# Converting float64 weights on ScalarE and VectorE alone, in pieces of 544 columns

## The chip, the core and the metric

The kernel runs on one core of a Trainium2 chip. The core's engines work side by side, each through its own list of instructions in order: TensorE (PE; its weight loads are shown apart as PEld), VectorE (DVE), ScalarE (ACT), GpSimd (POOL) and SyncE (SP), which here issues all transfers. They wait for each other by semaphores. The metric is the device time of one execution in microseconds.

## The reference

Attention with sketched features, and behind it one block that mixes tokens. `S1` and `S2` (8 x 32) and the four weight matrices of the second block come in as float64, `q`, `k`, `v` as float32.

```python
# B, H, S, D = 4, 4, 1088, 32; r = 8
def phi(x):                                   # 64 features of a token
    a, b = x @ S1.T, x @ S2.T
    return outer(a, b).reshape(64)
kv  = phi(k).T @ v                            # per batch and head
num = phi(q) @ kv
den = phi(q) @ sum(phi(k)) + 1e-6
x   = (num / den), heads side by side         # [B, 1088, 128]
theta = x @ w_theta
y   = w_tok_r @ (x * cos(theta)) + w_tok_i @ (x * sin(theta))   # over the 1088 tokens
u   = x + y
out = u + relu(u @ w_ch)
```

## The kernel before

Tokens are handled in 9 chunks of 128, three chunks to a group, so three groups a batch. For each batch, `keys(b)` cuts `k` and `q` into bfloat16 slices (`sl_k`, `sl_q`), sums `k k'` exactly, carries this through two more small products (their slices are `gsl`, `tsl`, `nsl`) into `rq`, with which the slices of `q` are multiplied later, and sums the features of `k` with `v` into `kvbd`. This is a long chain of small steps that goes to and fro between VectorE, ScalarE (casts, L196), GpSimd (remainders `r`, `r_c`) and TensorE. `queries(b, g)` works on a group: slices of `q` times `rq` give `lv` (ScalarE), then VectorE starts with `hi<-lv`, finds the denominator, the numerator, `x`, and theta's reduced angle (`tn`, `tt`), ScalarE takes sine and cosine, and `z` holds x cos and x sin. `mix(b, g)` multiplies all 17 tiles of `z` with a third of the columns of `wT`, the token weights (L509, product `y`), and finishes the output rows.

`wT` has 17 row blocks (`NK`) of 128 x 1088 float32. It is made once, at the beginning, from `w_tok`, which lies in memory as float64, by `load_f32` (L105). `load_f32` takes a piece of 272 columns (`part = S // 4`, so 68 pieces): a transfer brings the float64 words into a staging tile `st` (pool `stg`, six buffers); ScalarE takes the absolute value of each high word (L99) and turns the low word into a rounding step (L116, in place in `st`); VectorE clamps and shifts the magnitude (L84, twice); GpSimd adds the step as an integer (L80); VectorE masks a bit (L84) and puts the sign back from `st` (L87). `w2`, the two square matrices, goes the same way in one piece of 256 columns.

The program calls `tokens(20)` between the first batch's groups and the rest behind `keys(1)`, but that is not the order in which the engines run them: a scheduler of the compiler places every instruction in its engine's list by the costs and due times that it computes, and so the four VectorE passes of a piece stand far apart and among other work. It orders the transfers on SyncE's queue too. All buffers are handed out in turn, and a writer waits until the last reader of that buffer is done.

Of the kernel before, what the change touches and what calls it, by code (L numbers as in the profile page):

```python
"""Polysketch attention followed by the WaveMLP phase block, one launch on one core.

The float inputs that come in as float64 are handed to the chip as their bits (int64) and turned
into float32 there; S1 and S2 become pairs of float32.

The attention's denominator q' M q, M = S1' S1 (sum k k') S2' S2, comes close to zero, so it is
computed to about 2^-35 of its terms: every factor is cut into bfloat16 slices on a fixed grid, whose
products the tensor engine adds up exactly in float32, level by level (a level is the sum of
the two slices' numbers). Everything else is float32.
"""  # L10
# [9 lines left out]
F32 = mybir.dt.float32  # L20
BF16 = mybir.dt.bfloat16
I32 = mybir.dt.int32
U32 = mybir.dt.uint32
# [6 lines left out]
P = 128  # L30
EXPO = 0x7F800000          # a float32's exponent
SIGN = -(1 << 31)
SLICE = 1.5 * 2.0**17      # times 2^e: rounds values under 2^(e+1) to 8 bits and a sign
NL = 5                     # levels kept
ROUND = 1.5 * 2.0**23      # rounds to whole numbers
TWO_PI_A = 6.28125         # 2 pi, its first 8 bits and the rest
TWO_PI_B = 2.0 * math.pi - TWO_PI_A
PI_LOW = 3.1415925


@with_exitstack
def kernel(
    ctx: ExitStack,
    tc: tile.TileContext,
    q: bass.AP,       # [B, 128, NC, H, D], token 128 c + p, zeros behind the last
    k: bass.AP,
    v: bass.AP,
    s_t: bass.AP,     # [D, 2, R]: S1', S2'
    s_2: bass.AP,     # [R, D]: S2
    w_sq: bass.AP,    # [128, 2, 128]: w_theta, w_ch  # L50
    w_tok: bass.AP,   # [2 NF + 1, 128, S]: rows of w_tok_r', w_tok_i', and the last rows of both
    out: bass.AP,     # [B, S, 128]
):
# [12 lines left out]
    const = ctx.enter_context(tc.tile_pool(name="const", bufs=1))  # L66
    stg = ctx.enter_context(tc.tile_pool(name="stg", bufs=6))
    ld = ctx.enter_context(tc.tile_pool(name="ld", bufs=1))
# [10 lines left out]
    def tt(eng, o, a, b, op):  # L79
        eng.tensor_tensor(out=o, in0=a, in1=b, op=op)  # L80

    def ts(o, a, s1, op0, s2=None, op1=None):
        kw = {} if op1 is None else {"op1": op1}
        V.tensor_scalar(out=o, in0=a, scalar1=s1, scalar2=s2, op0=op0, **kw)  # L84

    def stt(o, a, s, b, op0, op1):
        V.scalar_tensor_tensor(out=o, in0=a, scalar=s, in1=b, op0=op0, op1=op1)  # L87
# [3 lines left out]

# [1 line left out]
    def split(t):  # L93
# [3 lines left out]
    def magnitude(h, hi):  # L97
        """The exponent and upper mantissa at float32's places, bits 30 and 31 not yet right."""
        A.activation(h, hi.bitcast(F32), AF.Abs)  # L99
        ts(h, h, 2.0**-15, ALU.max)  # L100
        x = h.bitcast(I32)
        ts(x, x, 3, ALU.logical_shift_left)
        return x

    def load_f32(dst, src):  # L105
        """dst [p, n] in SBUF = src, rounded to nearest."""
        p, n = dst.shape
        if src.dtype == F32:
            nc.sync.dma_start(dst, src)
            return  # L110
        st = stg.tile([P, n], I64, tag="st", name="st")[:p]
        nc.sync.dma_start(st, src)
        lo, hi = split(st)
        x = magnitude(dst, hi)
        # 2.0 + round(lo / 2^29) steps: its bits add the rounded low part and turn bit 30.
        A.activation(lo.bitcast(F32), lo.bitcast(U32), AF.Copy, bias=2.0, scale=2.0**-51)  # L116
        tt(G, x, x, lo, ALU.add)
        ts(x, x, 0x7FFFFFFF, ALU.bitwise_and)
        stt(x, hi, SIGN, x, ALU.bitwise_and, ALU.bitwise_or)

    def load_pair(src, n, tag, copies=1):
        """src as float32 pairs hi + lo, each [copies * p, n]."""
        p = src.shape[0]
# [23 lines left out]

# [1 line left out]
    ident = const.tile([P, P], F32, tag="ident", name="ident")  # L149
# [8 lines left out]
    def powers(m, n):  # L158
        """m [128, n], not negative: the greatest power of two up to each column's maximum."""
        t = psum(ps_acc, "acc")  # L160
        nc.tensor.transpose(t[:n, :P], m, ident)
        mx = sm.tile([P, 1], F32, tag="mx", name="mx")[:n]
        V.tensor_reduce(out=mx, in_=t[:n, :P], axis=AX.X, op=ALU.max)
        ts(mx.bitcast(I32), mx.bitcast(I32), EXPO, ALU.bitwise_and)
        dg = sm.tile([P, 2 * H], F32, tag="dg", name="dg")[:n, :n]
        ts(dg, ident[:n, :n], mx, ALU.mult)
        o = psum(ps_acc, "acc")
        nc.tensor.matmul(o[:, :n], ones[:n, :], dg, start=True, stop=True)
        s = sm.tile([P, 2 * H], F32, tag="pw", name="pw")[:, :n]
        V.tensor_copy(s, o[:, :n])  # L170
        return s

    def grids(pw, n, bits=8):
        """Numbers that round to the first and the second slice's grid."""
        g = sm.tile([P, 2, 2 * H], F32, tag="grid", name="grid")
        first = SLICE * 2.0 ** (8 - bits)
        ts(g[:, 0, :n], pw, first, ALU.mult)
        ts(g[:, 1, :n], pw, first * 2.0**-8, ALU.mult)
        return g
# [4 lines left out]
    def cut(cols, src, dst, r, g, lo=None, p=P):  # L184
        """Slices of src (+ lo). cols: (index into the grid, view) pairs, where view takes the
        part of a tile that has that scale; dst: the slices' tiles, r: a scratch tile."""
        for i, gi in ((0, 0), (1, 1)):
# [12 lines left out]
    def levels(src, n, by_head=False):  # L200
        """The sum hi + lo of the NL levels, src in PSUM: [p, NL, n], or [p, H, NL, n / H]."""
        lv = sm.tile([P, NL, n], F32, tag="lev", name="lev")
        A.copy(lv.rearrange("p l (h r) -> p h l r", h=H) if by_head else lv, src)
# [9 lines left out]

# [1 line left out]
    tiles = {}  # L215
# [6 lines left out]

# [1 line left out]
    load(0)  # L224
# [19 lines left out]
    V.tensor_copy(s1c, ssl[:, :, 0:R])  # L244
    # S2 with its rows on partitions: slices, and these four times side by side.
    s2sl = const.tile([P, NL, D], BF16, tag="s2sl", name="s2sl")[:R]
# [3 lines left out]
    for i in range(4):  # L250
        V.tensor_copy(s2x[:, :, i], s2sl)
    # S2' S2 by levels, its slices four times side by side.
    pp = psum(ps_acc, "acc")[:, :NL * D]
# [33 lines left out]

# [1 line left out]
    def keys(b):  # L289
# [15 lines left out]

        # Sums of k k' by slices: exact in the first ones.
        gp = psum(ps_acc, "acc")
# [13 lines left out]

        # (S1 C)' by levels, then N' = (S1 C P)'.
        tp = psum(ps_acc, "acc")[:, :H * NL * R]
# [57 lines left out]

# [1 line left out]
    def queries(b, g):  # L383
# [26 lines left out]

        # a . g, each cut into two slices of 11 bits on a grid of the token's own and a rest.
        def pair(x):
# [34 lines left out]

        # The numerator.
        qp = work.tile([P, CH, R, R], F32, tag="feat", name="qp")
# [20 lines left out]

        # theta, brought to [-pi, pi]; cos is sin(pi / 2 - |theta|).
        tr = psum(ps_tr, "tr")
# [5 lines left out]
        for i in range(GC):  # L478
            nc.tensor.matmul(th[:, i * P:(i + 1) * P], xT[:, i * P:(i + 1) * P], w2[:, 0],  # L479
                             start=True, stop=True)  # L480
        n_ = work.tile([P, GC * P], F32, tag="tn", name="tn")
        t_ = work.tile([P, GC * P], F32, tag="tt", name="tt")
        ts(n_, th, 1.0 / (2.0 * math.pi), ALU.mult, ROUND, ALU.add)
# [17 lines left out]

# [1 line left out]
    def mix(b, g):  # L503
# [25 lines left out]

# [1 line left out]
    load_f32(w2.rearrange("p t n -> p (t n)"), w_sq.rearrange("p t n -> p (t n)"))  # L531
    keys(0)
    queries(0, 0)
    part = S // 4
    pieces = [(i, n) for i in range(NK) for n in range(4)]

# [4 lines left out]

    tokens(20)
    queries(0, 1)
    tokens(20)
    queries(0, 2)
    tokens(20)
    load(1)
# [54 lines left out]
```

## Time and profile before

| | |
|---|---|
| median of 3 runs | 555.96 us (555.05 to 556.31) |
| span of the profiled execution, first to last instruction | 551.7 us |
| the profiled execution's own time | not recorded apart; the median is 4.3 us above the span |
| busy: TensorE / its weight loads | 338.5 us (61%) / 245.6 us (45%) |
| busy: VectorE / ScalarE / GpSimd | 393.4 us (71%) / 174.3 us (32%) / 164.7 us (30%) |
| mean granted TensorE clock | 0.759 |
| transfers | 28.93 MB, mean 52 GB/s |

Busy shares are averages over stages with different limits, so they say little by themselves. In the views, `out<-in` names the tiles an instruction writes and reads, L105 is line 105 of the kernel, "idle before" is the time in which the engine stood still ahead of an instruction, and the name behind the arrow is what ended it. In the tables of stretches, `(x30)` counts instructions and PEclk is the granted TensorE clock as a share of full speed.

### The profile page before, as it was taken

What the parts mean: (1) busy time and instruction counts of PE and PEld (TensorE: products, weight loads), DVE (VectorE), ACT (ScalarE), POOL (GpSimd) and SP (SyncE); (2) the same over time, 40 slices, a digit from 0 to 9 for tenths busy, and PEclk for the clock granted to TensorE, in tenths of its full rate; (3) what the DMA queues carried; (4) which work ended last, traced back from release to release, by engine and by line L of the source; (5) the groups of instructions that cost most, each with busy time, mean ns of one, the idle gap of its engine ahead of it and who ended that gap; (6) DMA issues with size and microseconds to landing.
All of it is one profiled execution on the core that took longest, in us unless ns stands there. A gap on an engine that the chain in (4) does not pass through costs nothing.

```text
span 551.7 us, 6346 instructions
## 1 busy us (share of the span) xinstructions
PE 338.5 (61%) x1971; PEld 245.6 (45%) x1971; DVE 393.4 (71%) x1207; ACT 174.3 (32%) x418; POOL 164.7 (30%) x209
## 2 busy tenths in 40 slices
PE   3212216345476625795677489956964997677696
PEld 2202106333354313564544357645644575545364
DVE  5988998888989989978679765186697541677311
ACT  3313443645635432304414221044144112234100
POOL 1315644453456524311321431021226110122000
PEclk9999555557676956697686669976687899586799
DMA  7022343542323542001001011000000000000000
GB/s 250 21 62 85 103 122 101 165 119 65 113 71 102 180 120 70 23 7 55 2 0 44 0 45 57 15 12 1 1 1 1 1 15 27 1 1 0 1 14 26
DMA packets 16513, 28.93 MB, mean 52 GB/s; under 512 B 1760, under 2 KB 6112, under 8 KB 16480
## 3 DMA queue, kind: packets, MB, share of 16 engines
q1 hardware_dynamic: 16480, 28.53, 16.8%
q8 instruction: 15, 0.25, 0.2%
q14 instruction: 18, 0.15, 0.1%
HBM read 26.30 MB, written 2.23 MB: 52 GB/s over the span
## 4 chain that ended last, share of the span: by engine, by line
DVE 43%; PE 33%; POOL 9%; issue 7%; ACT 5%; DMA 2%; SPq 1%; DVEq 0%; POOLq 0%; ACTq 0%
PE y L509 15%; DVE wT L84 8%; DVE wT L87 5%; DVE s L80 4%; POOL pr L80 4%; PE acc L366 4%; DVE r L80 3%; DVE qp L80 2%; PE mm L479 2%; POOL wT L80 2%; PE mm L518 2%; POOL r L80 2%; DVE sl_q L84 2%; DVE dn L441 2%; PE tr L474 1%
## 5 line engine op out<-in xcount | busy, mean ns | idle before, releaser
L509 PE MATMUL y<-wT,z 128*128 128x384 f32 (+1 forms) x408 | 159.0, 534 | 48.7 <-DVE z L80 30.5
L509 PEld LDWEIGHTS y<-wT,z 128*128 128x128 f32 x408 | 81.2, 213 | 90.2 <-DVE z L80 32.1
L84 DVE TENSOR_SCALAR wT<-wT 128x272 int32<-128x272 int32 (+1 forms) x204 | 78.2, 419 | 6.1 <-POOL wT L80 6.0
L80 POOL TENSOR_TENSOR wT<-wT,st 128x272 int32<-128x272 int32 x68 | 61.4, 912 | 69.9 <-DVE wT L84 43.7
L99 ACT ACTIVATE wT<-st 128x272 f32<-128x272 f32 x68 | 30.6, 449 | 37.4 <-DMA st<-w_tok 36.9
L80 DVE TENSOR_TENSOR uT<-xT,y 128x384 f32<-128x384 f32 (+1 forms) x12 | 6.3, 528 | 42.2 <-PE y L509 42.2
L80 POOL TENSOR_TENSOR z<-x,tt 128x384 f32<-128x384 f32 (+1 forms) x12 | 14.1, 1177 | 73.3 <-ACT tt L490 54.6
L87 DVE SCALAR_TENSOR_TENSOR wT<-st,wT 128x272 int32<-128x272 int32 x68 | 34.9, 520 | 0.0
L80 POOL TENSOR_TENSOR pr<-s 128x96 f32<-128x96 f32 x24 | 12.1, 505 | 72.2 <-DVE s L80 72.2
L462 PEld LDWEIGHTS mm<-kvbd,qpT 128*128 128x128 f32 x144 | 26.5, 257 | 12.8 <-ACT qpT L460 10.2
L460 ACT COPY qpT<-tr 128x256 f32<-128x256 f32 x36 | 13.3, 373 | 56.4 <-PE tr L456 55.8
L116 ACT ACTIVATE st<-st 128x272 f32<-128x272 uint32 (+1 forms) x69 | 30.6, 444 | 0.0
L456 PE MATMUL tr<-ident,qp 128*128 128x128 f32 x72 | 19.1, 386 | 18.5 <-DVE qp L80 11.7
L462 PE MATMUL mm<-kvbd,qpT 128*128 128x64 f32 x144 | 27.7, 340 | 2.2 <-ACT qpT L460 2.1
L311 PE MATMUL acc<-sl_k 128*128 128x128 bf16 x144 | 15.6, 293 | 20.2 <-ACT sl_k L196 20.2
L474 PE MATMUL tr<-ident,x 128*128 128x128 f32 x36 | 9.6, 396 | 29.6 <-DVE x L80 29.6
L441 DVE TENSOR_REDUCE dn<-pr 128x12 f32<-128x96 f32 (+2 forms) x36 | 12.7, 352 | 18.8 <-POOL pr L80 18.8
L80 POOL TENSOR_TENSOR kp<-ks 128x768 f32<-128x768 f32 x12 | 18.7, 1557 | 23.2 <-PE acc L366 16.5
L525 ACT ACTIVATE ot<-mm 128x384 f32<-128x384 f32 (+2 forms) x16 | 6.2, 408 | 60.6 <-PE mm L518 60.4
L456 PEld LDWEIGHTS tr<-ident,qp 128*128 128x128 f32 x72 | 13.8, 221 | 24.8 <-issue 15.7
L397 PE MATMUL mm<-rq,qT 128*128 128x72 bf16 x144 | 18.3, 211 | 9.4 <-ACT qT L394 4.6
L311 PEld LDWEIGHTS <-sl_k 128*128 128x128 bf16 x144 | 13.9, 138 | 21.4 <-ACT sl_k L196 20.7
(175 smaller groups left out, 763.8 us busy)
## 6 DMA issues: line engine op xcount, KB each, us to landing
st<-w_tok SPq DMA_DIRECT2D x68, 272.0 KB, 2.8
ld_k<-k_l SPq DMA_DIRECT2D x4, 576.0 KB, 3.8
ld_q<-q_l SPq DMA_DIRECT2D x4, 576.0 KB, 3.6
ld_v<-v_l SPq DMA_DIRECT2D x4, 576.0 KB, 3.8
out<-ot SPq DMA_DIRECT2D x8, 192.0 KB, 2.1
out<-ot SPq DMA_DIRECT2D x4, 128.0 KB, 1.8
st<-w_sq SPq DMA_DIRECT2D x1, 256.0 KB, 4.0
out<-ot SPq DMA_DIRECT2D x4, 32.0 KB, 1.8
```

What stands on the lines that cost most here:

```text
L80: eng.tensor_tensor(out=o, in0=a, in1=b, op=op)
L84: V.tensor_scalar(out=o, in0=a, scalar1=s1, scalar2=s2, op0=op0, **kw)
L87: V.scalar_tensor_tensor(out=o, in0=a, scalar=s, in1=b, op0=op0, op1=op1)
L99: A.activation(h, hi.bitcast(F32), AF.Abs)
L116: A.activation(lo.bitcast(F32), lo.bitcast(U32), AF.Copy, bias=2.0, scale=2.0**-51)
L311: nc.tensor.matmul(gp[:, h * P:(h + 1) * P], a, a, start=(c == 0 and h == 0), stop=(c == NC - 1), skip_group_check=True)
L366: nc.tensor.matmul(kv[:, n], kp[:, i * H + 2 * n:i * H + 2 * n + 2].rearrange("p h i j -> p (h i j)"), vn[:, c, 2 * n:2 * n + 2].rearrange ...
L397: nc.tensor.matmul(lp[:, h].rearrange("p l n -> p (l n)"), qT[:, h], rh[:, h, 0:3].rearrange("p l n -> p (l n)"), start=(h == 0), stop=Fal ...
L441: V.tensor_reduce(out=dn[:, j], in_=pr[:, :, j0:j1], axis=AX.XY, op=ALU.add)
L456: nc.tensor.transpose(tr[:, n * P:(n + 1) * P], qp[:, i * H + 2 * n:i * H + 2 * n + 2].rearrange("p h i j -> p (h i j)"), ident)
L462: nc.tensor.matmul(num[:, i * P + n * 2 * D:i * P + (n + 1) * 2 * D], qpT[:, n], kvbd[b % 2][:, n], start=True, stop=True)
L509: nc.tensor.matmul(yp[:, :w], z[:, i], wT[:, i, t0:t1], start=(i == 0), stop=(i == NK - 1))
```

## The change

`load_f32` does the conversion in five passes instead of seven, on pieces of 544 columns instead of 272 (34 instead of 68), and none of them is GpSimd's. ScalarE reads the staging tile three times: the high word scaled into `wT` (exponent and mantissa, its sign still on top), the high word scaled so far down that a float16 holds only its sign, written as the upper 16-bit half of a word in a new tile `step`, and the low word scaled and rounded to the lower 16-bit half of the same word. VectorE shifts `wT` left by three bits, which drops the sign and leaves room, and adds `step` as a 32-bit integer; the compiler makes of that addition an instruction on 16-bit halves (`ISA`, 1088 of them). `stg` has three buffers of twice the size, `step` two. To make room, `tn`, `tt` and `lev` go from two buffers to one. Comments are gone, which moves line numbers by 3 to 9: VectorE's helpers stand at L83, L87 and L90 for L80, L84 and L87, the three ScalarE passes at L124 to L126, the cast at L205.

```diff
-    stg = ctx.enter_context(tc.tile_pool(name="stg", bufs=6))
+    stg = ctx.enter_context(tc.tile_pool(name="stg", bufs=3))
...
     def load_f32(dst, src):
...
-        st = stg.tile([P, n], I64, tag="st", name="st")[:p]
+        st = stg.tile([P, PIECE], I64, tag="st", name="st")[:p, :n]
         nc.sync.dma_start(st, src)
         lo, hi = split(st)
-        x = magnitude(dst, hi)
-        # 2.0 + round(lo / 2^29) steps: its bits add the rounded low part and turn bit 30.
-        A.activation(lo.bitcast(F32), lo.bitcast(U32), AF.Copy, bias=2.0, scale=2.0**-51)
-        tt(G, x, x, lo, ALU.add)
-        ts(x, x, 0x7FFFFFFF, ALU.bitwise_and)
-        stt(x, hi, SIGN, x, ALU.bitwise_and, ALU.bitwise_or)
+        step = stg.tile([P, PIECE, 2], I16, tag="step", name="step", bufs=2)[:p, :n]
+        x = dst.bitcast(I32)
+        A.activation(dst, hi.bitcast(F32), AF.Copy, scale=2.0**-112)
+        A.activation(step[:, :, 1].bitcast(F16), hi.bitcast(F32), AF.Copy, scale=2.0**-60)
+        A.activation(step[:, :, 0], lo.bitcast(U32), AF.Copy, scale=2.0**-29)
+        ts(x, x, 3, ALU.logical_shift_left)
+        tt(V, x, x, step.rearrange("p n t -> p (n t)").bitcast(I32), ALU.add)
...
-        lv = sm.tile([P, NL, n], F32, tag="lev", name="lev")
+        lv = sm.tile([P, NL, n], F32, tag="lev", name="lev", bufs=1)
...
-        n_ = work.tile([P, GC * P], F32, tag="tn", name="tn")
-        t_ = work.tile([P, GC * P], F32, tag="tt", name="tt")
+        n_ = work.tile([P, GC * P], F32, tag="tn", name="tn", bufs=1)
+        t_ = work.tile([P, GC * P], F32, tag="tt", name="tt", bufs=1)
...
-    part = S // 4
-    pieces = [(i, n) for i in range(NK) for n in range(4)]
+    part = PIECE
+    pieces = [(i, n) for i in range(NK) for n in range(S // PIECE)]
...
-    tokens(20)
+    tokens(10)
     queries(0, 1)
-    tokens(20)
+    tokens(10)
     queries(0, 2)
-    tokens(20)
+    tokens(10)
     load(1)
```

The scheduler places everything anew, so more moves than the diff shows. Two places, with the tiles numbered as the compiler numbers them (`wT_316` is the one weight tile, `st_...` and `step_...` count up with the pieces).

On VectorE, the end of `queries(0, 0)` (from the first `x` to theta's angle `tn`, `tt`) and the beginning of `queries(0, 1)` (its `hi<-lv`). Before:

```order
L80 TENSOR_TENSOR x_757<-mm_733,rd_729 128x384
L84 TENSOR_SCALAR wT_316<-wT_316 128x272 x6
L87 SCALAR_TENSOR_TENSOR wT_316<-st_1182,wT_316 128x272
L84 TENSOR_SCALAR wT_316<-wT_316 128x272 x2
L87 SCALAR_TENSOR_TENSOR wT_316<-st_1191,wT_316 128x272
L87 SCALAR_TENSOR_TENSOR wT_316<-st_1200,wT_316 128x272
L84 TENSOR_SCALAR wT_316<-wT_316 128x272 x2
L84 TENSOR_SCALAR tn_768<-mm_764 128x384
L84 TENSOR_SCALAR wT_316<-wT_316 128x272
L84 TENSOR_SCALAR tn_768<-tn_768 128x384
```

After (`step_1655` belongs to the last of the 34 pieces):

```order
L83 TENSOR_TENSOR x_756<-mm_732,rd_728 128x384
L87 TENSOR_SCALAR wT_316<-wT_316 128x544 x2
L83 ISA wT_316<-wT_316,step_1639 128x1088
L83 ISA wT_316<-wT_316,step_1647 128x1088
L87 TENSOR_SCALAR wT_316<-wT_316 128x544
L87 TENSOR_SCALAR tn_767<-mm_763 128x384
L83 ISA wT_316<-wT_316,step_1655 128x1088
L87 TENSOR_SCALAR tn_767<-tn_767 128x384
L90 SCALAR_TENSOR_TENSOR tt_768<-tn_767,mm_763 128x384
L90 SCALAR_TENSOR_TENSOR tt_768<-tn_767,tt_768 128x384
L87 TENSOR_SCALAR tt_768<-tt_768 128x384
L83 TENSOR_TENSOR hi_923<-lv_859 128x288
```

Before, the pieces go on behind this place through `queries(0, 1)`, `queries(0, 2)` and `keys(1)`; now the last one ends inside `queries(0, 0)`, and `keys(1)` is spread over the first batch's remaining groups as the later batches' keys are.

On ScalarE, in `keys(0)`, around the casts of `tsl` and the copy of the next product's levels (`lev`), both in the chain to `rq`. Before:

```order
L99 ACTIVATE wT_316<-st_942 128x272
L116 ACTIVATE st_942<-st_942 128x272
L196 CAST tsl_477<-r_c_494 128x32 x3
L99 ACTIVATE wT_316<-st_951 128x272
L116 ACTIVATE st_951<-st_951 128x272
L203 COPY lev_517<-acc_511 128x160
```

After:

```order
L126 ACTIVATE step_1075<-st_1073 128x544
L205 CAST tsl_476<-r_c_493 128x32
L124 ACTIVATE wT_316<-st_1081 128x544
L205 CAST tsl_476<-r_c_493 128x32
L125 ACTIVATE step_1083<-st_1081 128x544
L205 CAST tsl_476<-r_c_493 128x32
L126 ACTIVATE step_1083<-st_1081 128x544
L124 ACTIVATE wT_316<-st_1241 128x544
L212 COPY lev_516<-acc_510 128x160
```

The three casts followed each other; now a pass over a piece of twice the size stands between each two, and another ahead of the copy.

More of the change, by code (lines that the diff above doesn't have):

```diff
@@ L21 @@
 BF16 = mybir.dt.bfloat16
+F16 = mybir.dt.float16
+I16 = mybir.dt.int16
 I32 = mybir.dt.int32
@@ L38 @@
 PI_LOW = 3.1415925
+PIECE = 544
 @with_exitstack
```

## The prediction

> **What bounds the kernel now.** I read the page for the totals, then cut the span at the first VectorE instruction of each batch's queries (`hi<-lv` of `queries(b, 0)`), because every batch runs the same program from one such point to the next, and only the first batch has the conversion of the token weights inside it. The cuts are these rows of the timeline of VectorE (start, length):
>
> ```profile
> 103.00 0.44 DVE L80 TENSOR_TENSOR hi<-lv 128x288 f32<-128x288 f32 x1
> ...
> 254.06 0.44 DVE L80 TENSOR_TENSOR hi<-lv 128x288 f32<-128x288 f32 x1
> ...
> 363.52 0.45 DVE L80 TENSOR_TENSOR hi<-lv 128x288 f32<-128x288 f32 x1
> ...
> 468.51 0.46 DVE L80 TENSOR_TENSOR hi<-lv 128x288 f32<-128x288 f32 x1 [2.98 <-ACT lv L403]
> ```
>
> At these cuts the busy time of each engine by stretch is, first for all instructions, then for those on `wT` alone (the last block ends with the sum over the span):
>
> ```profile
> core 0: us, PE busy (x) PEld busy (x) DVE busy (x) ACT busy (x) POOL busy (x), PEclk, DMA share, GB/s
> 0.00:35.20 35.20, 9.92 (x41) 7.80 (x41) 26.63 (x160) 11.03 (x35) 8.07 (x17) 1.00 0.33 113
> 35.20:103.00 67.80, 19.38 (x154) 17.00 (x154) 61.05 (x183) 26.29 (x64) 32.42 (x31) 0.64 0.38 114
> 103.00:254.10 151.10, 89.77 (x493) 63.25 (x493) 133.18 (x388) 61.77 (x151) 63.00 (x76) 0.71 0.30 90
> 254.10:363.50 109.40, 79.65 (x490) 58.32 (x490) 71.03 (x200) 29.28 (x66) 25.83 (x32) 0.77 0.07 22
> 363.50:468.50 105.00, 78.93 (x487) 57.50 (x487) 64.13 (x184) 29.58 (x66) 24.87 (x32) 0.80 0.02 6
> 468.50:551.70 83.20, 60.83 (x306) 41.70 (x306) 37.39 (x99) 16.35 (x37) 10.56 (x21) 0.78 0.02 7
> ...
> 0.00:35.20 35.20, 0.00 (x0) 0.00 (x0) 2.88 (x7) 2.65 (x6) 1.54 (x2) 1.00 0.33 113
> 35.20:103.00 67.80, 0.00 (x0) 0.00 (x0) 34.88 (x90) 9.22 (x21) 19.88 (x22) 0.64 0.38 114
> 103.00:254.10 151.10, 45.14 (x102) 21.20 (x102) 71.58 (x176) 18.68 (x42) 39.94 (x44) 0.71 0.30 90
> ...
> sum 551.70, PE 159.01 PEld 81.17 DVE 109.34 ACT 30.55 POOL 61.36; mean PE 26.50 PEld 13.53 DVE 18.22 ACT 5.09 POOL 10.23
> ```
>
> The first batch takes 151.1 us, the second and third, with the same keys, queries and mixing, 109.4 and 105.0. VectorE is busy for 133 of the 151 us, 71.6 of them on the weights; without these it would have 61.6 us of work, close to the 71.0 and 64.1 of the next batches. So the first batch is VectorE's, and the surplus of 42 to 46 us is the weights'. The chain that ended last says it too, for 103 to 254 and for 363.5 to 468.5:
>
> ```profile
> by line: DVE wT L84 21.2%; DVE wT L87 10.7%; issue 9.6%; PE y L509 5.3%; POOL wT L80 4.5%; DMA st<-w_tok 4.1%; POOL pr L80 3.3%; PE acc L366 2.9%; DVE qp L80 2.8%; DVE s L80 2.7%; PE mm L518 2.3%; DVE r L80 2.2%; DVE tn L84 2.2%; DVE z L80
> ...
> by line: PE y L509 26.6%; DVE s L80 5.8%; DVE r L80 5.0%; POOL pr L80 4.7%; PE acc L366 4.2%; PE mm L479 3.6%; DVE qp L80 3.0%; DVE tt L87 2.7%; POOL r L80 2.4%; DVE sl_q L84 2.4%; issue 2.4%; PE mm L518 2.3%; PE mm L462 2.2%; PE tr L474 2.
> ```
>
> Weight conversion and its transfers hold 40% of the first chain and none of the second. TensorE pays at the end: the token mixing waits for the last pieces, and ScalarE for their transfers (waits from 103 to 254, total and times; the last row is the last piece):
>
> ```profile
> PE y L509 <- DVE wT L87: 18.2, 5, 12.3
> ...
> ACT wT L99 <- DMA st<-w_tok: 25.7, 17, 3.3
> ...
> 229.94 0.43 DVE L87 SCALAR_TENSOR_TENSOR wT<-st,wT 128x272 int32<-128x272 int32 x1
> ```
>
> **The change, part by part.** Prices of one instruction, from the trace (rows with a bar give busy us and mean ns, then idle time before them; rows with two strokes give least, median and largest ns):
>
> ```profile
> L84 DVE TENSOR_SCALAR wT<-wT 128x272 int32<-128x272 int32 (+1 forms) x204 | 78.2, 419 | 6.1 <-POOL wT L80 6.0
> ...
> L84 DVE TENSOR_SCALAR wT<-wT x204: 278/291/2443, 14.6 to 228.3; 128x272 int32<-128x272 int32 x68, 128x272 f32<-128x272 f32 x34
> ...
> L84 DVE TENSOR_SCALAR tt<-tt x12: 346/356/1549, 125.4 to 516.4; 128x384 f32<-128x384 f32 x12
> ...
> L80 DVE TENSOR_TENSOR r<-r,gsl 128x512 f32<-128x512 f32 x4 | 2.8, 690 | 0.1
> L80 DVE TENSOR_TENSOR r<-r,sl_k 128x1152 f32<-128x1152 f32 x4 | 5.4, 1358 | 0.0
> ...
> L196 ACT CAST gsl<-r 128x512 bf16<-128x512 f32 x12 | 7.4, 619 | 13.4 <-POOL r L80 8.5 <-DVE r L80 4.9
> L196 ACT CAST sl_k<-r 128x1152 bf16<-128x1152 f32 x8 | 9.2, 1154 | 20.5 <-POOL r L80 11.5 <-DVE r L80 9.0
> ...
> L116 ACT ACTIVATE st<-st 128x272 f32<-128x272 uint32 (+1 forms) x69 | 30.6, 444 | 0.0
> ```
>
> *VectorE.* Four passes on each of 68 pieces of 272 go (109.3 us busy, sum row). Two on each of 34 pieces of 544 come. The shift: 291 ns at 272 elements and 356 at 384 is 0.58 ns an element, so 0.45 us at 544. The addition has no row: it adds words as two 16-bit halves (1088 of them). Its ends are 0.72 us, as 544 elements with two inputs (690 ns at 512, 1358 at 1152, so 1.04 ns each), and 1.29 us, as 1088. I take 0.72: it reads and writes as many bytes as the 544-element row, and that size is the nearer one. [...] A piece is then 1.17 us (bounds 1.17 and 1.74), all pieces 40 us (59), and VectorE has 69 us (50) less to do.
>
> *GpSimd.* Its 61.4 us on `wT` go. VectorE's weight passes stood idle only 6.0 us for them (first row), so I count no time, only that the shift's 2443 ns maximum against a 291 ns median should become rarer; the other GpSimd work stays and can still delay VectorE.
>
> *ScalarE.* Two passes of 272 become three of 544. The casts give 619 ns at 512 and 1154 at 1152, 0.84 ns an element, so 0.65 us at 544; from the 444 ns at 272 it is 0.67. I take 0.67, 2.0 us a piece, 68 us for all against 61 before (30.6 twice). The bounds are 0.65 and, if a pass that writes every other 16-bit half ran at half rate, 1.1 us, so 1.95 to 2.9 us a piece.
>
> *Transfers.* 34 of 544 KB for 68 of 272 KB, three staging buffers for six. The nearest rows:
>
> ```profile
> st<-w_tok SPq DMA_DIRECT2D x68, 272.0 KB, 2.8
> ...
> ld_q<-q_l SPq DMA_DIRECT2D x4, 576.0 KB, 3.6
> ```
>
> A buffer used to be held until the last VectorE pass; now the third ScalarE pass frees it. It turns in 3.6 us (landing) plus 2.0 us, plus up to some 2 us behind other ScalarE work: 5.6 to 7.6 us for three pieces, 1.9 to 2.5 us a piece. That, and not VectorE, is now the pace of the weights. The other edits (`tn`, `tt`, `lev` with one buffer instead of two) I cost at nothing: the next writer comes a whole group of chunks later, when the readers are long done; were that cover gone, a group would wait for one reader of 384 columns, less than the 1.15 us of the 1152-column cast above.
>
> *Where the pieces stand.* This decides what VectorE's 69 us are worth. Counted over VectorE's order, 23 of the 68 small pieces are finished ahead of the first cut (`hi` of `queries(0, 0)`), and after the change 26 of the 34 large ones: from 34% of the elements to 76%. So the stretch up to 103 us gets no relief. VectorE's weight work there was 37.8 us (2.88 and 34.88) and becomes 26 x 1.17 = 30; ScalarE's was about 24 (twice 2.65 and 9.22) and becomes 52 of the 103 us, its passes standing between the casts of the keys' slices, on which `rq` and then `hi` depend. From 35 us, with three pieces done, 23 more at 1.9 to 2.5 us take 44 to 58 us, to 79 to 93, and the end of the keys' chain follows: the old 68 us just about hold. I take 104 us for the cut, with bounds of 96 (VectorE's 7 us come through) and 113 (each piece also waits for a cast, 2.9 us).
>
> The first batch then has 8 pieces left, all ahead of its first `tn`, and otherwise the program of the second and third: 107 us, the mean of 109.4 and 105.0. The 8 pieces cost VectorE 9.4 us; a third of its time is idle in the second batch (71 of 109), so I take 6 us. Bounds are 105 (all hidden) and 125 (8 x 2.0 us of ScalarE all on the path of the slower batch). So 113 us instead of 151.
>
> *The sum.* 104 + 113 + the remaining 297.6 us (551.7 less 254.1), which hold no changed instruction, are 515 us of span. The median of the runs, 555.96, is 4.3 us above the span of the profiled execution, which I add: 519 us, 37 us less. By the slow addition (0.57 us more for 34 pieces, 19 us of VectorE) with everything on the path it would be 538.
>
> **The rivals.**
> *The slow addition.* At 1.29 us VectorE's work up to the first cut is 87.7 - 37.8 + 26 x 1.74 = 95 of 104 us, fuller than VectorE was in the old first batch (133 of 151), so that waits show: I give it 7 us there and 3 in the batch, 529 us.
> *ScalarE and the ring become the bound.* For it speaks that three passes go to an engine that has the critical casts in line behind them. If a pass takes 1.1 us, a piece takes 3.0 to 3.5 us, 23 of them 69 to 80 us from 35 on, the cut comes at 115 to 120, and the time is 530 to 535 us. Against it speaks that ScalarE was busy for 37 of the first 103 us only. [...]
> *Slower than before.* One mechanism: the ring of three. With 23 pieces at p us from 35 us on and some 5 us of keys' chain behind them, the cut comes at 40 + 23 p; with the batch of 113 us it reaches the old 254 us at p = 4.4 us. That needs a turn of 13 us for three pieces, of which 3.6 are a landing: landings would have to be three times as long. At my pace the stretch from 35 us to the cut moves 23 pieces of 557 kB and two loads of 590, about 205 GB/s; this execution has moved 250 in its first slice:
>
> ```profile
> GB/s 250 21 62 85 103 122 101 165 119 65 113 71 102 180 120 70 23 7 55 2 0 44 0 45 57 15 12 1 1 1 1 1 15 27 1 1 0 1 14 26
> ```
>
> *Relief up to the cut.* If the keys' chain gets VectorE's 7 us and the 8 pieces hide: 96 + 106 + 297.6 + 4.3 = 504 us.
> *Hidden anyway.* If TensorE's granted clock (0.71 in the first batch) and not VectorE made the 151 us, the time stays. Against it: TensorE is busy for 90 of them, as against 79 of 105 later.
>
> **How the numbers follow.** The forecast (513 to 525 us) 0.52; relief (500 to 513) 0.17; slow addition or ScalarE's pace (525 to 538) 0.22; slower 0.05, hidden 0.02, and 0.02 for a gain beyond 500. The predicted time is the first case's 519. The range takes in relief and both slow cases: 502 to 537. A measurement of this kernel can tell 0.2% from no change. Faster 0.93, same 0.02, slower 0.05.
>
> **What will show it.** The last weight piece should be finished near 118 us, not 230; the cuts should stand near 104, 217, 325 and 431 us. The addition's row decides 0.72 or 1.29, ScalarE's three rows 0.67, the landing of 544 KB 3.6. ScalarE's waits for the weights' transfers should grow up to the first cut. I am wrong if the first cut moves past 115 us, or if the first batch stays above 125 us after its weights are done, since then it was not VectorE's weight work that made it long.

## The result, and the profile after

| | before | after |
|---|---|---|
| median of the runs | 555.50 us (554.43 to 556.31) | 519.66 us (518.27 to 520.44) |
| ratio | | 0.935 (0.933 to 0.937) |
| span of the profiled execution | 551.7 us | 516.5 us (its own time 518.27) |

The prediction said 519 us, 502 to 537. The same cuts as before, from VectorE's timeline of the changed kernel (start, length), with the last piece of the weights between them:

```profile
103.68 0.45 DVE L83 TENSOR_TENSOR hi<-lv 128x288 f32<-128x288 f32 x1
...
126.72 0.71 DVE L83 CUSTOM_DVE_ANT_0 wT<-wT,step 128x1088 uint16<-128x1088 uint16 x1
...
218.59 0.45 DVE L83 TENSOR_TENSOR hi<-lv 128x288 f32<-128x288 f32 x1
...
327.94 0.45 DVE L83 TENSOR_TENSOR hi<-lv 128x288 f32<-128x288 f32 x1
...
433.20 0.46 DVE L83 TENSOR_TENSOR hi<-lv 128x288 f32<-128x288 f32 x1 [2.99 <-ACT lv L412]
```

The busy time of each engine between these cuts, for all instructions and then for those on `wT` alone:

```profile
core 0: us, PE busy (x) PEld busy (x) DVE busy (x) ACT busy (x) POOL busy (x), PEclk, DMA share, GB/s
0.00:35.20 35.20, 10.19 (x41) 7.89 (x41) 27.02 (x162) 17.67 (x41) 5.56 (x14) 1.00 0.54 171
35.20:103.70 68.50, 20.20 (x157) 17.79 (x157) 56.22 (x147) 52.34 (x87) 12.75 (x9) 0.63 0.64 203
103.70:218.60 114.90, 78.78 (x490) 57.24 (x490) 77.77 (x216) 44.99 (x90) 25.19 (x32) 0.77 0.15 46
218.60:327.90 109.30, 81.94 (x490) 60.00 (x490) 69.64 (x199) 29.41 (x66) 24.76 (x32) 0.77 0.07 22
...
0.00:35.20 35.20, 0.00 (x0) 0.00 (x0) 3.42 (x6) 4.31 (x7) 1.00 0.54 171
35.20:103.70 68.50, 0.00 (x0) 0.00 (x0) 30.02 (x47) 14.17 (x21) 0.63 0.64 203
103.70:218.60 114.90, 37.73 (x102) 19.72 (x102) 10.61 (x16) 4.83 (x7) 0.77 0.15 46
```

The whole gain lies in the first batch: 114.9 us instead of 151.1. The first cut has moved by 0.7 us, and what follows the first batch takes 297.9 us instead of 297.6. In the first batch VectorE now has 10.6 us of weight work instead of 71.6 and is busy for 78 of 115 us, much as in the second (70 of 109). Up to the first cut, VectorE's weight work (3.4 and 30.0 us) is about what it was, as more pieces stand there, and ScalarE is busy twice as long as before (52 us instead of 26 from 35 us on). The prices of the passes (least, median, largest ns) and of a transfer:

```profile
L124 ACT ACTIVATE wT<-st x34: 665/692/718, 10.7 to 118.6; 128x544 f32<-128x544 f32 x34
L87 DVE TENSOR_SCALAR wT<-wT x34: 421/430/444, 11.9 to 124.1; 128x544 int32<-128x544 int32 x34
L83 DVE CUSTOM_DVE_ANT_0 wT<-wT,step x34: 657/720/2890, 15.4 to 126.7; 128x1088 uint16<-128x1088 uint16 x34
...
L125 ACT ACTIVATE step<-st x35: 473/811/842, 9.4 to 124.9; 128x544 f16<-128x544 f32 x34, 128x256 f16<-128x256 f32 x1
...
L126 ACT ACTIVATE step<-st x35: 460/797/822, 9.7 to 125.6; 128x544 int16<-128x544 uint32 x34, 128x256 int16<-128x256 uint32 x1
...
st<-w_tok SPq DMA_DIRECT2D x34, 544.0 KB, 4.6
```

Two things are left to explain: what holds the first stretch at 103.7 us, and which part of the change made the batch short. The chain of work that ended last, for 34 to 104 us before and for 35 to 104 us after:

```profile
by line: issue 20.9%; DVE wT L84 16.8%; DVE wT L87 13.8%; PE acc L366 11.3%; POOL wT L80 6.2%; POOL r L80 5.1%; DVE r L80 4.9%; DVE gsl L84 3.4%; DVE sl_q L84 2.8%; POOL r_c L80 1.8%; ACT sl_k L196 1.7%; PE acc L168 1.6%; DVE lev L80 1.5%; 
...
by line: DMA st<-w_tok 13.5%; POOL r L83 12.7%; PE acc L375 11.3%; ACT step L126 9.8%; ACT step L125 9.5%; DVE wT L83 4.8%; ACT wT L124 4.4%; DVE sl_k L87 4.0%; issue 3.7%; DVE r L83 3.7%; ACT sl_q L205 3.2%; ACT gsl L205 2.5%; DVE wT L87 2
```

Before, VectorE's and GpSimd's passes on the weights held 37% of it; now the weights' transfers and ScalarE's passes hold 37%, VectorE's passes some 7%. A chain names only the wait that ended last at each step, so it does not say what would come earlier if one of them were left out.

My theory was the prediction's: the first stretch goes by the ring of three buffers and ScalarE's passes, the batch by VectorE's passes. The rival was that VectorE holds both, so that the first stretch pays for every piece that stands in it.

### The profile page after: what moved, and what is told of

Read it like the earlier page. It is cut to its first block, busy times and chain, and to the rows that moved or that the text cites. A ratio compares the mean times of both kernels' runs of the same rounds, so it can differ in the third digit from the quotient of the medians.

```text
span 516.5 us, 5795 instructions
## 1 busy us (share of the span) xinstructions
PE 331.7 (64%) x1971; PEld 242.7 (47%) x1971; DVE 332.3 (64%) x1001; ACT 190.2 (37%) x385; POOL 103.6 (20%) x140
## 4 chain that ended last, share of the span: by engine, by line
PE 40%; DVE 36%; ACT 9%; POOL 9%; DMA 3%; issue 3%; SPq 1%; DVEq 0%; POOLq 0%
PE y L518 20%; DVE s L83 5%; POOL pr L83 4%; PE acc L375 4%; DVE r L83 4%; POOL r L83 3%; PE mm L488 3%; DVE qp L83 2%; DVE dn L450 2%; PE mm L527 2%; DMA st<-w_tok 2%; DVE sl_k L87 2%; PE tr L483 2%; ACT step L126 1%; DVE wT L83 1%
## 5 line engine op out<-in xcount | busy, mean ns | idle before, releaser
L518 PE MATMUL y<-wT,z 128*128 128x384 f32 (+1 forms) x408 | 155.6, 528 | 23.1 <-DVE z L83 23.1
L83 DVE TENSOR_TENSOR uT<-xT,y 128x384 f32<-128x384 f32 (+1 forms) x12 | 6.4, 530 | 53.6 <-PE y L518 53.6
L83 DVE CUSTOM_DVE_ANT_0 wT<-wT,step 128x1088 uint16<-128x1088 uint16 x34 | 30.4, 898 | 8.9 <-ACT step L126 8.8
L471 PEld LDWEIGHTS mm<-kvbd,qpT 128*128 128x128 f32 x144 | 28.6, 275 | 14.5 <-ACT qpT L469 10.8
L469 ACT COPY qpT<-tr 128x256 f32<-128x256 f32 x36 | 13.2, 372 | 53.6 <-PE tr L465 53.1
L83 POOL TENSOR_TENSOR pr<-s 128x96 f32<-128x96 f32 x24 | 12.0, 498 | 103.7 <-DVE s L83 103.7
L465 PE MATMUL tr<-ident,qp 128*128 128x128 f32 x72 | 19.4, 393 | 20.5 <-DVE qp L83 10.2
L83 POOL TENSOR_TENSOR z<-x,tt 128x384 f32<-128x384 f32 (+1 forms) x12 | 14.8, 1231 | 85.8 <-ACT tt L499 56.3
L471 PE MATMUL mm<-kvbd,qpT 128*128 128x64 f32 x144 | 29.1, 355 | 3.2 <-ACT qpT L469 3.1
L125 ACT ACTIVATE step<-st 128x544 f16<-128x544 f32 (+1 forms) x35 | 28.0, 800 | 4.8 <-DVE pw L179 3.1
L126 ACT ACTIVATE step<-st 128x544 int16<-128x544 uint32 (+1 forms) x35 | 27.6, 788 | 0.0
L83 POOL TENSOR_TENSOR kp<-ks 128x768 f32<-128x768 f32 x12 | 19.4, 1620 | 40.5 <-PE acc L375 23.3
L124 ACT ACTIVATE wT<-st 128x544 f32<-128x544 f32 x34 | 23.3, 688 | 9.8 <-DMA st<-w_tok 9.4
L485 ACT COPY xT<-tr 128x384 f32<-128x384 f32 x12 | 5.7, 478 | 54.4 <-PE tr L483 54.4
L87 DVE TENSOR_SCALAR tn<-mm 128x384 f32<-128x384 f32 x12 | 6.7, 557 | 28.5 <-PE mm L488 28.5
```

Of the source, the lines that this page charges most:

```text
L124: A.activation(dst, hi.bitcast(F32), AF.Copy, scale=2.0**-112)
L125: A.activation(step[:, :, 1].bitcast(F16), hi.bitcast(F32), AF.Copy, scale=2.0**-60)
L126: A.activation(step[:, :, 0], lo.bitcast(U32), AF.Copy, scale=2.0**-29)
L465: nc.tensor.transpose(tr[:, n * P:(n + 1) * P], qp[:, i * H + 2 * n:i * H + 2 * n + 2].rearrange("p h i j -> p (h i j)"), ident)
L471: nc.tensor.matmul(num[:, i * P + n * 2 * D:i * P + (n + 1) * 2 * D], qpT[:, n], kvbd[b % 2][:, n], start=True, stop=True)
L518: nc.tensor.matmul(yp[:, :w], z[:, i], wT[:, i, t0:t1], start=(i == 0), stop=(i == NK - 1))
```

## The experiments

"First cut" and "first batch" are the first two stretches of the profile of each kernel, in us; the later stretches differ from those after by at most 2 us unless said. Ratios are to the kernel before.

| kernel | time | ratio | first cut | first batch |
|---|---|---|---|---|
| changed kernel | 519.66 | 0.935 (0.933 to 0.937) | 103.7 | 114.9 |
| one pass a piece | 498.97 | 0.897 (0.894 to 0.900) | 86.2 | 114.1 |
| addition on GpSimd | 529.12 | 0.953 (0.951 to 0.954) | 115.1 | 116.1 |
| pieces of 272, six buffers | 509.97 | 0.917 (0.916 to 0.919) | 95.0 | 116.2 |
| old passes, pieces of 544 | 543.62 | 0.978 (0.976 to 0.981) | 109.0 | 135.7 |
| two staging buffers | 513.56 | 0.926 (0.923 to 0.929) | 97.7 | 116.4 |
| before, single tn, tt, lev | 555.76 | 1.000 (0.998 to 1.002) | 103.2 | 153.1 |
| added matmuls | 517.63 | 0.933 (0.930 to 0.936) | 103.0 | 115.7 |
| 272, six buffers, added matmuls | 507.57 | 0.914 (0.911 to 0.917) | 95.1 | 111.9 |
| no VectorE passes | 500.04 | 0.900 (0.898 to 0.901) | 90.5 | 110.2 |
| one step pass | 517.33 | 0.930 (0.928 to 0.932) | 106.6 | 113.0 |
| 272, three buffers | 505.33 | 0.908 (0.907 to 0.910) | 94.3 | 112.0 |
| 272, two buffers | 523.29 | 0.944 (0.941 to 0.946) | 93.3 | 136.1 |

**One pass a piece.** Only the first ScalarE pass is left.

```diff
-        A.activation(step[:, :, 1].bitcast(F16), ...)
-        A.activation(step[:, :, 0], ...)
-        ts(x, x, 3, ALU.logical_shift_left)
-        tt(V, x, x, step..., ALU.add)
```

> Leaves out: the rounding step and the sign (ScalarE's second and third pass) and both VectorE passes; only the scaled high word is written to the weights, transfers and their buffers stay. It measures what the conversion still costs. My theory (up to the first cut, the first VectorE instruction of queries(0,0), ScalarE's passes and the ring of three buffers pace the keys' chain): the weights' passes and transfers held 45% of the chain between 35 and 103.7 us, 31 us; the first cut goes from 104 to 75-88 us, the first batch from 115 to 105-109, and the time from 520 to 490-500. Rival (the keys' chain alone takes that long, the pieces are hidden in it): first cut at 98 us or later, time 505-514.

The first cut came 17.5 us earlier, the batch 0.8. So the new conversion still costs something, nearly all of it ahead of the first cut. With only four ScalarE passes of the weights left in it, the first batch still takes 114 us and not 107.

**The addition on GpSimd.**

```diff
-        tt(V, x, x, step..., ALU.add)
+        tt(G, x, x, step..., ALU.add)
```

> The addition goes back to GpSimd (34 of about 1.8 us, from 912 ns at 272 columns), all else as after: 61 us more of GpSimd, 30 us less of VectorE. My theory (the gain is VectorE's relief in the first batch, GpSimd counts nothing): first cut 104 +-4 us, first batch 113-117 us, time 515-524. Rival (the gain came from freeing GpSimd, whose instructions hold up VectorE's): first batch back above 125 us, time above 530.

It cost 9.5 us, between the two. The batch hardly changed; the first cut came 11.4 us later, although VectorE had 18 us less weight work ahead of it. VectorE and GpSimd up to the first cut, changed kernel and then this one, each for all and for `wT`:

```profile
0.00:103.70 103.70, 30.39 (x198) 25.68 (x198) 83.24 (x308) 70.01 (x127) 18.31 (x23) 0.76 0.61 192
...
0.00:103.70 103.70, 0.00 (x0) 0.00 (x0) 33.44 (x53) 18.48 (x27) 0.76 0.61 192
```

```profile
0.00:115.10 115.10, 30.42 (x198) 25.97 (x198) 88.54 (x286) 70.75 (x129) 53.24 (x50) 0.76 0.54 174
...
0.00:115.10 115.10, 0.00 (x0) 0.00 (x0) 15.76 (x26) 18.51 (x28) 36.86 (x26) 0.76 0.54 174
```

VectorE's other work is 49.8 us in 255 instructions in the first and 72.8 us in 260 in the second. Some got longer while GpSimd added: the three `dg` of 4 x 4 took 1169 ns in the mean, and each ended within 0.03 us of an addition. One such pair from the two timelines (GpSimd first, then VectorE on a 4 x 4 tile), and the mean of the same VectorE instruction in the changed kernel, where GpSimd does not add:

```profile
93.30 1.34 POOL L83 TENSOR_TENSOR wT<-wT,step 128x544 int32<-128x544 int32 x1 [0.74 <-DVE mx L87]
...
93.25 1.40 DVE L87 TENSOR_SCALAR dg<-ident,mx 4x4 f32<-4x4 f32 x1
```

```profile
L87 DVE TENSOR_SCALAR dg<-ident,mx 4x4 f32<-4x4 f32 x12 | 2.6, 214 | 0.2
```

The small instruction ended when GpSimd's did (94.64 and 94.65 us), 1.2 us late, and it stands in the keys' chain: 1.40 for 0.21 us, beside a 1.34 us addition (by the records VectorE's began 0.05 us ahead). What holds the two together was not shown. So to keep the addition off GpSimd, which I had counted at nothing, is worth 9.5 us in this kernel, its longer way through the chain included.

**Old passes on pieces of 544, and new passes on pieces of 272.** Together they split the change in two. The first is the kernel before with three staging buffers, pieces of 544 and single `tn`, `tt`, `lev`; the second is the changed kernel with

```diff
-PIECE = 544
+PIECE = 272
-    stg = ... bufs=3
+    stg = ... bufs=6
-        step = ... bufs=2
+        step = ... bufs=4
-    tokens(10)
+    tokens(20)
```

> The old seven passes with GpSimd, on pieces of 544 with three staging buffers; tn, tt and lev with one buffer, as after. VectorE 34 x (3 x 0.43 + 0.71) = 68 us plus its waits, for 109 before and 44 after. My theory (VectorE's weight work in the first batch decides): about 19 pieces of 34 are left at the first cut, 38 us of VectorE for 10, so the first batch takes 130-140 us and the time is 535-545. Rival (piece size alone made the gain): 518-526. Rival (piece size is worth nothing): 552-558.

> The new five passes on pieces of 272, six staging and four step buffers, as many bytes in flight. VectorE 68 x (0.29 + 0.43) = 49 us for 44, ScalarE 68 x (0.45 + 0.52 + 0.52) = 101 for 75. My theory (fewer passes on VectorE made the gain, ScalarE paces the first stretch): first cut 105-115 us, time 521-535. Rival (larger pieces made the gain, by fewer instructions and transfers): time near 545-556.

The old passes on large pieces gained 12 us (109.0 and 135.7), the new passes the other 24: with them the batch lost 21 us more, as VectorE's and GpSimd's passes left it. The second missed: small pieces were better by 9.7 us, with the first cut at 95.0. Their passes cost more in sum (the three of ScalarE 0.43, 0.50 and 0.49 us at 272), so the price of a pass isn't what decides. What had changed is the order: 59% of VectorE's weight instructions now stand ahead of the first cut (81 of 136) instead of 78% (53 of 68). That spoke for the rival, but only by the count. The row of `wT` up to the first cut with small pieces:

```profile
0.00:95.00 95.00, 0.00 (x0) 0.00 (x0) 33.07 (x81) 16.89 (x41) 0.78 0.55 173
```

VectorE spends as long on the weights there as in the changed kernel (33.1 and 33.4 us), and still the cut comes 8.7 us earlier. So the sum of VectorE's passes ahead of the cut does not set it alone. The passes are shorter and stand in other places; no run separates the two.

**Two staging buffers.** `bufs=2` for `stg` in the changed kernel; 38 of 68 stand ahead.

> The changed kernel with two staging buffers instead of three; the scheduler then puts 19 pieces of the weights ahead of the first cut instead of 26, and 15 in the first batch instead of 8. Theory (the first stretch pays for the number of pieces that stand in it, 17.5 us for 26, and the first batch takes them for next to nothing): 7 pieces fewer are worth about 5 us, first cut at 97 to 100 us, first batch 115 to 118, time 512 to 517 us. Rival (the pace of the ring, transfers of 4.6 us and then three passes): two buffers turn in 3.3 to 4 us a piece, ScalarE's queue stands in front of the transfers with the keys' casts behind it, the first cut stays at 104 or comes later, time 520 to 530 us, with ScalarE's waits for the weights' transfers up from 5.6 us to over 15.

A slower ring made the kernel 6.1 us faster. ScalarE waited longer for transfers (11.1 instead of 5.6 us from 35 to 104 us), and still the cut came 6 us earlier and the batch took 1.5 us more. So the turn of the ring alone is not the pace: with seven large pieces fewer ahead of it, the first cut comes earlier in spite of the longer waits.

**The kernel before with single `tn`, `tt` and `lev`.**

> The kernel before with only tn, tt and lev cut to one buffer. My prediction counts this at nothing: 554 to 557 us, all cuts within 1 us of the old ones. Rival (a reader holds the only buffer for up to 1.15 us in each of 12 groups): 560 to 569 us, spread evenly over the batches.

No difference in time: 555.76 against 555.86 us. The first cut is within 0.2 us of the old one, the later three 2 to 3 us behind; but the profiled execution has a span of 554.7 us, the one before of 551.7, so that is scatter as far as the times show.

**Added matmuls.** The granted clock drops to 0.5 at 53 us in the changed kernel, behind 15.2 us without work on TensorE (up to 46.4 us), and stayed at 1.0 until 120 us in the kernel with one pass. That could have been part of its 17.5 us.

```diff
+        if b == 0:
+            yw = psum(ps_y, "y")
+            for i in range(10):
+                nc.tensor.matmul(yw[:H], gk[:, 0, :H], ...512 columns of kn..., start=True, stop=True)
```

> The changed kernel with ten float32 matmuls of 512 columns added on TensorE after the keys' grid, results unused, so that it is busy from 33 to 45 us, where it stood idle for 15 us. Nothing moves on VectorE or ScalarE. Theory (the idle gap makes the granted clock fall to 0.5 from 53 to 126 us, and that is a part of what the first stretch takes over the 86 us of the kernel without rounding and sign): the clock stays near 1.0 past 100 us, the keys' key features take 4 us instead of 7.8, the first cut comes at 95 to 100 us, time 510 to 516 us. Rival (the first stretch is held by VectorE and ScalarE alone, the clock only follows how little TensorE has to do): clock at 0.5 as before or 1.0 without any gain, first cut 103 to 104 us, time 518 to 521 us.

> The kernel with the new passes in pieces of 272 (six staging, four step buffers, 510.0 us) with the same ten added matmuls. Theory (clock): first cut at 88 to 92 us instead of 95, time 502 to 507 us, faster than every kernel so far that computes everything. Rival: 509 to 511 us; it would say that the gain of smaller pieces and that of the clock are the same thing.

The row of the clock fell all the same (0.50 from 55 to 120 us in both), and the first cuts stayed (103.0 and 95.1). By themselves these two runs neither show the theory nor refute it: behind the added matmuls TensorE still stood idle for 3.8 us (with small pieces for 2.2 of the 13 us up to 46 us), and its work from 70 to 110 us was no faster than without them (98 matmuls in 14.9 us for 94 in 14.0; with small pieces 111 in 18.2 for 112 in 18.3). The kernel with one pass speaks against it: its 36 matmuls of the key features take 422 ns in the mean, against 420 in the changed kernel, though its row shows 1.00, so a faster clock at these matmuls is no part of its 17.5 us. In the later batches the same matmuls take 275 ns in the median; what that speed would give the first stretch was not measured. The small-piece kernel had a batch 4 us shorter than without; but the intervals of the ratios overlap (0.916 to 0.919 and 0.911 to 0.917), the profiled executions are the fastest of their four with the matmuls and the slowest without, and I leave this open.

**No VectorE passes, and one step pass.** The first leaves the shift and the addition out and keeps ScalarE's three passes; the second writes the step in one 32-bit pass.

```diff
-        ts(x, x, 3, ALU.logical_shift_left)
-        tt(V, x, x, step..., ALU.add)
```

```diff
-        A.activation(step[:, :, 1].bitcast(F16), ...)
-        A.activation(step[:, :, 0], lo.bitcast(U32), ...)
+        A.activation(step....bitcast(I32), lo.bitcast(U32), AF.Copy, scale=2.0**-29)
```

> The changed kernel without VectorE's shift and addition (the weights stay as the first ScalarE pass leaves them); ScalarE's three passes and the transfers stay, 26 pieces ahead of the first cut. It tells whose work the 17.5 us are that the first stretch has over the kernel with one pass. Theory (VectorE: 30 us of passes in a stretch where it is busy for 56 of 68 us): first cut at 86 to 92 us, time 499 to 507 us. Rival (ScalarE: 42 us of added passes stand between the keys' casts): first cut at 98 to 104 us, time 512 to 520 us. Between them, the two share it.

> The changed kernel with one pass instead of two for the step (rounded low part as a 32-bit word, the sign left out), so ScalarE has two passes a piece; the scheduler then puts some 30 pieces ahead of the first cut. If ScalarE's passes hold the first stretch, 0.80 us a piece less bring the first cut to 88 to 96 us, time 503 to 512 us. If VectorE's do, four more pieces of 1.15 us make it 103 to 108 us, time 519 to 524 us.

The first gives shares, in this order of leaving out: the cut at 90.5 us is 13.2 us earlier than with VectorE's passes and 4.3 later than without ScalarE's added ones. The second decides less: ScalarE's work up to the cut fell from 70 to 56 us, and the cut came 2.9 us later, with VectorE's weight instructions up from 53 to 61; the time, 517.3 us, is below the range for VectorE and above that for ScalarE, by a batch of 113.0. The cut lies in VectorE's range, but ScalarE's waits for the weights' transfers from 35 to 104 us grew at the same time, changed kernel and then one step pass:

```profile
ACT wT L124 <- DMA st<-w_tok: 5.6, 6, 2.0
...
ACT wT L124 <- DMA st<-w_tok: 13.7, 14, 2.2
```

With shorter passes the ring of three buffers showed more of its transfers, 8 of the 14 us that ScalarE had less to do. So the cut may be late by the ring as well as by VectorE. The rows for 35 us to the cut, first and second, with ScalarE nearly as full in the first as its stretch is long:

```profile
35.20:90.50 55.30, 20.33 (x157) 17.87 (x157) 32.22 (x103) 47.05 (x80) 9.54 (x9) 0.65 0.72 226
```

```profile
35.20:106.60 71.40, 20.45 (x157) 17.96 (x157) 58.22 (x156) 42.87 (x75) 13.23 (x9) 1.00 0.70 229
```

So VectorE's passes are the largest share of the first stretch that a run shows, 13.2 us or 0.4 us for each of their 33.4; ScalarE's passes and the ring have a part that these runs bound only from one side. The row of the clock is 0.65 for the shorter stretch and 1.00 for the longer, with 20.3 and 20.5 us of TensorE, so the clock does not make the difference between these two.

**Fewer small pieces ahead.** Three and two staging buffers of 272 instead of six: 67 and 50 of 136 weight instructions ahead of the first cut.

> Pieces of 272 with three staging buffers instead of six (four step buffers): 67 of 136 VectorE weight instructions ahead of the first cut instead of 81. Theory (the first stretch pays per piece, the first batch has room): 14 instructions fewer at 0.34 to 0.43 us bring the first cut from 95.0 to 89 to 91 us, the first batch takes 116 to 119 us, time 504 to 509 us against 510. Rival (the ring of three small buffers holds ScalarE's queue, or the batch is full): first cut at 95 or later, or batch of over 122 us, time over 511 us.

> Pieces of 272 with two staging buffers instead of three: 50 of 136 VectorE weight instructions ahead of the first cut instead of 67, so 8.5 small pieces fewer. Theory (VectorE's passes cost the first stretch 13.2 us for 26 large pieces, so 0.25 us a small one): first cut 2 us earlier, at 92 us, first batch 112 to 115 us, time 502 to 506 us. Rival (with two buffers the transfer of 2.9 us shows between the passes, ScalarE waits over 20 us for them ahead of the first cut, or the last piece comes later than 174 us and the mixing waits for it): first cut at 95 or later, or batch over 117 us, time 508 us or more.

With three the time is inside the theory's range and the best of all that convert fully, 14 us under the changed kernel. But the first cut gained 0.7 us, not 5, though VectorE's weight work ahead of it fell from 33.1 to 28.5 us, and the batch took 4.2 us less than with six, which I don't explain (the profiled executions are the fastest of their four with three buffers and the slowest with six). With two the theory failed: the cut at 93.3 is 1.0 us earlier for another 8.2 us of VectorE's weight work, and the batch took 136. So with small pieces the first stretch hardly pays by their number any more. The last pieces in the two timelines, three buffers and then two:

```profile
173.91 0.43 DVE L83 CUSTOM_DVE_ANT_0 wT<-wT,step 128x544 uint16<-128x544 uint16 x1
```

```profile
209.58 0.43 DVE L83 CUSTOM_DVE_ANT_0 wT<-wT,step 128x544 uint16<-128x544 uint16 x1
```

ScalarE's waits behind the first cut with two buffers, and its total over the run in the page's groups:

```profile
ACT wT L124 <- DMA st<-w_tok: 18.5, 21, 1.5
...
L124 ACT ACTIVATE wT<-st 128x272 f32<-128x272 f32 x68 | 30.3, 445 | 29.9 <-DMA st<-w_tok 29.9
```

Here the ring did become the pace, at the other end: the last piece ends 36 us later than with three buffers. Some of the first batch's products with `wT` then come late (9.4 us of them stand between 210 us and the cut at 229.4), and the batch is 24 us longer; the stretches behind give 6 us back (104.7 and 102.6 us for 107.8 and 105.3). TensorE was slower there too: 24 matmuls of the next batch's key features took 5.31 us instead of 2.82. There is an optimum: few pieces ahead of the first cut, but the last one done early enough. Kernels that convert fully with the new passes and end the last piece at 174 us or before have batches of 112 to 116 us; at 210 us it is 136. The limit lies between.

## Why the prediction was right, and where its steps were not

*The first batch, 113 us: 114.9.* Right, and by the mechanism named: VectorE's 61 us of weight work left it. GpSimd's 39.9 us on the weights left it too, which the prediction counted at nothing, and no run separates the two: with 12.1 us of them back (the addition on GpSimd) the batch is 1.2 us longer. Nor does every microsecond count: with 25.5 us of VectorE's weight work in it (pieces of 272, three buffers) the batch takes 112.0 us. The split into 107 and 6 was wrong. With one pass a piece the batch still takes 114.1 us, without VectorE's passes 110.2, so VectorE's share of the eight pieces is at most about 5 us, and the rest was not the mean of the later batches. What separates 110 from 114 us I did not find.

*The first cut, 104 us: 103.7.* The number held by luck, its working did not hold. I made the ring and ScalarE "the pace of the weights" and VectorE's 7 us a possible relief. The chain does go by the transfers and ScalarE's passes for 37%, but two buffers moved the cut forward, and leaving VectorE's passes out moved it by 13.2 us, so the ring does not set it alone. The step that failed is the pace of 1.9 to 2.5 us a piece: from 35 us to the cut VectorE finished 23.5 pieces (47 instructions) in 68.5 us, 2.9 us each. Two of its prices were low as well, ScalarE's passes (0.69, 0.81 and 0.80 us for 0.67) and the landing (4.6 us for 3.6). The upper bound of 113 us does not follow either: 2.9 us a piece gives 107 by the prediction's own 40 + 23 p. That the cut stayed where it was is a sum of opposite changes: up to it VectorE's weight work fell from 37.8 to 33.4 us, GpSimd's 21.4 us went (an addition put back there cost 11.4 us), and ScalarE's weight work rose from 24 to 58.5 us. How these cancel was not measured.

*The addition, 0.72 us: a median of 0.72*, so the rival of 1.29 us falls. The mean is 0.90, as some take longer; the two longest, 2.54 and 2.89 us, overlap a subtraction of GpSimd's on the key slices.

*GpSimd at nothing:* wrong by the experiment above, 9.5 us for the addition alone. The row I had read, 6.0 us of idle time behind GpSimd, shows only waits for its results; what an instruction takes longer beside GpSimd's work stands in the busy time, as with `dg`, 1.40 us busy and 0.21 without the addition.

*Single buffers at nothing:* right. *The rest, 297.6 us:* 297.9. *The time outside the span, 4.3 us:* the median is 3.2 us above this span. In every execution whose own span is on record the time is 1.7 to 2.0 us above it, so the rest of the 4.3 us must be that the profiled execution had been faster than the median. The sum came to 519 with errors of one to two microseconds that nearly cancel.

*Signs named ahead:* the cuts at 104, 217, 325 and 431 came at 103.7, 218.6, 327.9 and 433.2, the last piece at 126.7 instead of 118. ScalarE's waits for the weights' transfers up to the first cut should have grown; they fell, from 11.1 to 7.0 us. ScalarE was busier there (70 us instead of 37), which would explain it but was not tested apart.

The rival of relief (504 us) was not this kernel's. Pieces of 272 come near its number, 505 to 510 us with the cut at 94 to 95, but not by its mechanism: VectorE's weight work up to the cut is no less with six buffers.

## What to carry to other kernels

Work that is hidden in an in-order queue can still delay the chain that shares the queue: count how much of it stands ahead of the first point that others wait for, and try to move that count (by buffers, or piece size). Here it gave 6 us with large pieces and next to nothing with small ones, so neither the count nor the sum of the busy time is enough to forecast it. A short row of waits on GpSimd does not show what GpSimd costs VectorE (6.0 us of waits in the kernel before; 9.5 us of time for the addition alone); compare the busy time of the same VectorE instructions with and without it. The chain that ended last named the transfers and ScalarE, and leaving out VectorE's passes still gained 13.2 of 17.5 us; look at both before calling a stretch one engine's. When a run leaves out or shortens one engine's passes, look at what else moved (pieces ahead, waits for transfers) before reading it as a share.

## What was not expected of the hardware

The row of the granted clock in the first stretch told nothing of the speed there. The four executions of the changed kernel had mean clocks of 0.776, 0.846, 0.843 and 0.773, with spans of 516.5, 518.3, 518.7 and 517.5 us. The same 36 matmuls of the key features and `v`, in the changed kernel while the row showed 0.50, and in the kernel with one step pass while it showed 1.00:

```profile
L375 PE MATMUL acc<-ld_v,kp x36: 314/421/475, 86.3 to 93.9; 128*128 128x64 f32 x36
```

```profile
L374 PE MATMUL acc<-ld_v,kp x36: 314/421/475, 90.2 to 97.8; 128*128 128x64 f32 x36
```

Their medians are the same, 421 ns. In the later batches, where the row also shows 1.00 (from 406 to 413 us), the same 36 have a median of 275 ns; 24 of them, as the chain shows them from 327.9 to 433 us in the changed kernel, take 2.82 us instead of the 5.31 of the first batch:

```profile
406.12 2.82 PE acc L375 x24
```

So TensorE was slow in the first batch whatever the row showed, and alike in five kernels: the 36 took 423 ns in the mean before, 420 in the changed kernel, 422 with one pass, 420 with one step pass, 423 with single `tn`, `tt` and `lev`. The durations count, not the row. Nor does the row go with the 36 products of `sl_k`: they took 4.02 us behind a gap of 12.4 us in the kernel with one pass and 3.71 us behind 15.2 us in the changed kernel, both with 1.00 over the gap and the products, and 3.45 us behind 3.8 us in the kernel with the added matmuls, with 0.61. With small pieces and the added matmuls TensorE did 37 matmuls in 2.28 us from 46 to 50 us, and the row shows 1.00. What made TensorE slow in the first batch was not shown.

ScalarE's passes that write every other 16-bit half took 0.81 and 0.80 us, against 0.69 for one that writes whole words, at 544 elements: 16 to 17% more, far from double. In the kernel with one step pass the same low words, written as whole words, took 682 ns in the mean of 35, of which one has 256 elements, so about 0.69 us at 544.
